# Attention's output matmuls in alternation with the piece next to them on TensorE

## The chip, the cores and the metric

The kernel runs on one core of a Trainium2 chip. The metric is the device time of one execution in microseconds (us); lower is better. Shorter times are in nanoseconds (ns).

## What is computed

Grouped-query attention followed by a feed-forward layer with a squared ReLU. There are 8 batches of 384 positions, 16 query heads on 4 key and value heads, and a head dimension of 64:

```
scores = q @ k.T / sqrt(64)                 # per batch and head, 384 x 384
attn   = exp(scores - max) / (sum(exp(scores - max)) + 1e-9)
x      = attn @ v                            # heads side by side: 3072 x 1024
h      = maximum(x @ w_in, 0)                # 1024 -> 2048
out    = (h * h) @ w_out                     # 2048 -> 1024
```

Inputs and output are float32; the kernel multiplies in 16-bit types.

## The kernel before

**Engines and recorder.** All work goes through `R.add(engine, fn, reads, writes, ...)` of the class `Recorder` (lines 22 to 170). It finds what an operation depends on and keeps it in one list; `emit` (L124) then writes each engine's operations in the order of their recording, a wait on semaphores before an operation and one increment at its last instruction. Loops that plan ahead (from about line 1640 on) choose what TensorE gets next, from modelled times at which operands and PSUM banks come free. So the order on TensorE (PE) is fixed when the kernel is built.

**Batches.** While the feed-forward layer of batch b runs on PE, attention of batch b + 1 runs between its pieces. Three kinds of piece matter:

- *score*, in `burst_small` (matmuls at L471): q times k for one or two key tiles, 512 or 256 columns, into two PSUM banks; ScalarE (ACT) takes the exponential from there (L481).
- *up* and *down*, built by `zipped` (matmuls at L926 for the first matrix, at L968 for the second; an older form of them, for batch 0, is at L634 and L1302). Both use a scheme of seven products for a 2 x 2 split. A piece has mostly eight matmuls, of 192 columns (up) or 512 (down).
- *attention's output*, in `av_halves` (matmuls at L538), for batches 1 to 6. For one pair of heads' results there are 36 matmuls, in two operations of 18, the halves: `mm(pe, 0)` and `mm(pe, 1)`. One matmul takes 65 columns: 64 of v, and a column of ones that gives the sum for the softmax. After the second half DVE takes the reciprocal (L551) and multiplies (L553), and the result goes by a transposing DMA (L558) to the next layer.

**Row halves.** Nearly all of these matmuls use 64 of the 128 rows of PE's array: half 0 or half 1, by the partitions that the operands are on. In the instruction order they alternate between the halves, so that two run side by side. A sum over 128 rows is made in two passes into the same PSUM bank: what half 0 has begun in a bank, half 1 continues later, and the other way round. The second waits by semaphore until the first has landed (`after=(lead,)` in `av_halves`, `lead` in `zipped`), so PE has waits on itself.

The two halves of an attention output, in the kernel before, order their matmuls by bank:

```
for x in range(2):
    f, h = 6 * s2 + NJ * x + n, (x + y) % 2
```

The first operation (y = 0) is 0, 1, 0, 1 in row halves, the second (y = 1) is 1, 0, 1, 0.

Of the kernel before, what the change touches and what calls it, by code (L numbers as in the profile page):

```python
# [8 lines left out]
class Tally:  # L9
# [5 lines left out]
    def __getattr__(self, name):  # L15
        def count(*args, **kwargs):
            self.n += 1
            return self
        return count


class Recorder:
# [37 lines left out]
            t = max(t, o["end"])  # L60
        return t

    def add(self, eng, fn, reads=(), writes=(), dma=None, cost=0.1, issue=0.1, shared=(), after=(), port=False):
        i = len(self.ops)
        deps = self.deps_of(reads, writes)
        raw = {self.writer[r] for r in reads if r in self.writer}
        for r in reads:
            self.readers.setdefault(r, []).append(i)
        for w in writes:
            self.writer[w] = i  # L70
            self.readers[w] = []
        need = set(after)
        for d in deps:
            o = self.ops[d]
            if o["dma"] is None and o["eng"] == eng and dma is None:
                if eng in self.IN_ORDER or d not in raw:
                    continue
            need.add(d)
        if dma is not None:
            if dma in self.dma_last:  # L80
                need.add(self.dma_last[dma])
            self.dma_last[dma] = i
        start = max([self.clock[eng]] + [self.ops[d]["end"] for d in need])
        if dma is not None:
            self.clock[eng] = start + issue
            if eng == "gpsimd":
                self.pool.append((start, start + 0.3 * issue))
            q = eng
            begin = max(self.ring.get(q, 0.0), start + issue + 0.8)
            if shared and begin > start + issue + 0.8:  # L90
                shared = (3.0, shared[1])
            if shared and self.ring.get("gpsimd", 0.0) > begin:
                self.ring["gpsimd"] += shared[1]
                for o in self.ops:
                    if o["eng"] == "gpsimd" and o["dma"] is not None and o["end"] > begin:
                        o["end"] += max(0.0, min(shared[1], o["end"] - 1.2 - begin))
                cost = shared[0]
            self.ring[q] = begin + cost
            kind = dma.rstrip("0123456789z_")
            lag, work = self.WIRE.get(kind, (2.2, 1.25))  # L100
            self.wire = max(self.wire, start + lag) + work
            end = begin + cost + (1.5 if begin > 30 else 1.2 if eng == "gpsimd" else 0.7)
        else:
            if eng == "gpsimd":
                self.pool.append((start, start + cost))
            elif port:
                cost += max([0.0] + [z - start for a, z in self.pool[-6:] if a <= start < z])
            self.clock[eng] = start + cost
            if eng == "tensor":
                fn(self.tally)  # L110
                self.marks.append((start + cost, self.tally.n))
            end = start + cost + (0.2 if eng == "tensor" else 0.07)
        self.ops.append(dict(eng=eng, fn=fn, dma=dma, need=need, signal=False, start=start, end=end))
        return i

    def emit(self):
        nc, ops = self.nc, self.ops
        for o in ops:
            for d in o["need"]:
                ops[d]["signal"] = True  # L120
        sems = {e: nc.alloc_semaphore(f"done_{e}") for e in self.ENGINES}
        count = {}
        for o in ops:
            if o["dma"] is not None:  # L124
                s = self.dma_sems.get(o["dma"])
                if s is None:
                    s = self.dma_sems[o["dma"]] = nc.alloc_semaphore(f"dma_{o['dma']}")
                key, step = ("dma", o["dma"]), 16
            elif o["signal"]:
                s, key, step = sems[o["eng"]], o["eng"], 1  # L130
            else:
                o["at"] = None
                continue
            count[key] = count.get(key, 0) + step
            o["at"] = (key, count[key])
            o["sem"] = s
        known = {e: {} for e in self.ENGINES}
        for o in ops:
            k = known[o["eng"]]
            waits = {}  # L140
            for d in sorted(o["need"], reverse=True):
                key, v = ops[d]["at"]
                if k.get(key, 0) >= v:
                    continue
                waits[key] = (ops[d]["sem"], v)
                for kk, vv in ops[d]["know"].items():
                    if k.get(kk, 0) < vv:
                        k[kk] = vv
                if k.get(key, 0) < v:
                    k[key] = v  # L150
            o["waits"] = [w for w in waits.values()]
            o["know"] = dict(k)
            if o["at"] is not None:
                o["know"][o["at"][0]] = max(o["know"].get(o["at"][0], 0), o["at"][1])
        with nc.Block() as block:
            for e in self.ENGINES:
                mine = [o for o in ops if o["eng"] == e]

                def body(eng, mine=mine):
                    for o in mine:  # L160
                        for s, v in o["waits"]:
                            eng.wait_ge(s, v)  # L162
                        last = o["fn"](eng)
                        if o["at"] is not None:
                            last.then_inc(o["sem"], 16 if o["dma"] is not None else 1)

                getattr(block, e)(body)

# [3 lines left out]
def bass_gqa_attention__then__ffn_squared_relu_kernel(  # L172
# [14 lines left out]
    NJ = S // 128  # L187
# [17 lines left out]
    R = Recorder(nc)  # L205
# [258 lines left out]
    def burst_small(b, pieces, base):  # L464

        n, c0, wide = slot(b, pieces[0][0]), pieces[0][1], pieces[0][2]

        def sc(pe):
            for m, (u, _, _) in enumerate(pieces):
                for x in range(2):  # L470
                    mm = pe.matmul(ps[:, base + x, m * wide:(m + 1) * wide],  # L471
                                   kT[at(b)][64 * x:64 * x + 64, u, :], q_cols(b, u // NJ, x, c0, c0 + wide))
            return mm

        total = wide * len(pieces)
        keys = [("bank", base), ("bank", base + 1)]
        R.add("tensor", sc, reads=[r for p in pieces for r in score_reads(b, *p)], writes=keys,
              cost=total / 2400 + (0.004 if b else 0.2))
        src = ps[:, base:base + 2, 0:total].rearrange("p x (k c) -> p x k c", k=len(pieces))
        dst = expT[n // 6][:, n % 6:n % 6 + len(pieces), :, c0:c0 + wide].rearrange("p k x c -> p x k c")  # L480
        R.add("scalar", lambda e: e.activation(dst, src, AF.Exp, scale=0.125), reads=keys,  # L481
              writes=[("expT", slot(b, u), t) for u, _, _ in pieces
                      for t in range(c0 // 128, (c0 + wide) // 128)], cost=(0.2 if b else 0.07) + total / 600)
# [41 lines left out]
    def av_halves(b, c, pairs):  # L525

        g, s2 = c // 2, c % 2
# [3 lines left out]
        def mm(pe, y):  # L531
            for n in range(NJ):
                for j in range(NJ):
                    for x in range(2):
                        f, h = 6 * s2 + NJ * x + n, (x + y) % 2
                        r = slice(64 * h, 64 * h + 64)
                        w = unit_of(b, g * NJ + j)[r, f % 2, (f // 2) * 128:(f // 2) * 128 + 128]
                        m = pe.matmul(ps[:, p[x], n * DP:n * DP + D + 1], w, v_aug[b % 2][r, g * NJ + j, 0:D + 1],  # L538
                                      start=(n + j + y == 0), stop=(n + j + y == 2 * NJ - 1))
            return m  # L540

        keys = [("bank", i) for i in p]
        lead = R.add("tensor", lambda pe: mm(pe, 0), reads=av_reads(b, c), writes=keys, cost=0.275)
        yield lead
        held.difference_update(p)
        R.add("tensor", lambda pe: mm(pe, 1), reads=av_reads(b, c), writes=keys, cost=0.275, after=(lead,))
        r = (b * 8 + c) % 2
        o = o_slot(b, g)
        po = ps[:, p[0]:p[0] + 2, 0:NJ * DP].rearrange("p s (i e) -> p s i e", i=NJ)
# [285 lines left out]
    def zipped(ups, lows):  # L835
# [15 lines left out]
        def piece():  # L851
            def mm(pe):
                for _, _, m in todo:
# [2 lines left out]

            held.update(first)
            i = R.add("tensor", mm, reads=need, writes=[("bank", x) for x in sorted({h.bank for h in halves})], cost=cost,
                      after=tuple(e[0] for h in halves for e in h.lead))
            for h in halves:  # L860
                if h.done:
                    h.done(i)
# [1166 lines left out]
```

## Time and profile before

| | |
|---|---|
| median of 3 runs | 395.71 us (394.32 to 395.84) |
| the profiled execution | 395.19 us, its span 393.4 us |
| PE matmuls | 387.3 us busy, 98% of the span, 7019 instructions |
| PE weight loads | 302.6 us, 77% |
| VectorE (DVE) | 308.3 us, 78% |
| ScalarE (ACT) | 272.2 us, 69% |
| GpSimd (POOL) | 144.6 us, 37% |
| granted TensorE clock | 0.999 |

A line of a group reads: source line, engine, operation, what is written and read, partitions x elements and type, the count; then the busy time in us, the mean of one in ns, and the idle time ahead of it with what ended it. `64*128 64x65` is a matmul over 64 rows and 128 columns of the array with 65 columns streamed through. PEld stands for the weight loads, which run beside the matmuls. Matmuls overlap: 190 ns is the time of one from start to end, not the distance between two. In a timeline the columns are start (us from the span's start), duration (us), engine, line, operation and operands; rows that follow each other closely are merged with a count.

### The profile page before, as it was taken

The numbers are of one execution on the slowest core, as the hardware profiler recorded it, in microseconds if no ns is written. First come the engines' busy times: TensorE is split into PE (matmuls) and PEld (weight loads), VectorE is DVE, ScalarE is ACT, GpSimd is POOL, SyncE is SP. The second block draws the span as 40 slices with busy tenths as digits, with TensorE's granted clock in tenths as the row PEclk, the third lists the DMA queues.
The fourth block names the chain that finished last, engine by engine and source line by source line (L and its number), as shares of the span: only waits on it lengthen the run. The fifth ranks groups of instructions, "written<-read, shape, count | busy, mean of one in ns | idle before, by whom it ended". The sixth has DMA issues, their size and how long they took to land. (4 is left out here: it accounts for less than half of the span.)

```text
span 393.4 us, 15642 instructions
## 1 busy us (share of the span) xinstructions
PE 387.3 (98%) x7019; PEld 302.6 (77%) x7022; DVE 308.3 (78%) x646; ACT 272.2 (69%) x397; POOL 144.6 (37%) x168
## 2 busy tenths in 40 slices
PE   8999999999999999999999999999999999999996
PEld 6565674455555899799977999899987899799653
DVE  3689788889989988888886688898885688856642
ACT  5948999689845897778882587978782297436511
POOL 7756420044002563466422243525301144126111
PEclk9999999999999999999999999999999999999999
DMA  9999999995329975884788318976712223120023
GB/s 168 182 197 188 207 200 181 147 258 82 42 77 125 188 103 79 126 158 77 107 125 186 105 25 73 139 145 83 83 49 102 86 45 25 48 82 4 28 82 107
DMA packets 95635, 44.40 MB, mean 113 GB/s; under 512 B 75984, under 2 KB 89552, under 8 KB 95568
## 3 DMA queue, kind: packets, MB, share of 16 engines
q0 software_dynamic: 36672, 17.44, 35.3%
q1 hardware_dynamic: 58080, 25.40, 32.4%
q8 instruction: 55, 0.90, 1.0%
q10 hardware_dynamic: 816, 0.56, 0.5%
q14 instruction: 12, 0.10, 0.1%
HBM read 35.65 MB, written 12.58 MB: 123 GB/s over the span
## 5 line engine op out<-in xcount | busy, mean ns | idle before, releaser
L481 ACT ACTIVATE expT<-ps 128x1024 bf16<-128x1024 f32 (+1 forms) x124 | 121.0, 1015 | 25.4 <-PE ps L471 25.1
L968 PE MATMUL ps<-w_out_sb,h2T 64*128 64x512 f16 x528 | 98.0, 376 | 0.0
L926 PE MATMUL ps<-xT,w_in_sb 64*128 64x192 f16 x1152 | 84.4, 243 | 0.3 <-DVE y_sb L1126 0.2
L926 PEld LDWEIGHTS ps<-xT,w_in_sb 64*128 64x128 f16 x1152 | 70.7, 94 | 3.0 <-PE ps L926 0.7
L823 POOL TENSOR_TENSOR h2T<-hr 128x384 f16<-128x384 f32 x55 | 44.8, 834 | 53.3 <-ACT hr L811 53.2
L968 PE MATMUL ps<-area,xT 64*128 64x512 f16 x288 | 55.7, 376 | 0.0
L926 PE MATMUL ps<-s_all,wx 64*128 64x192 f16 x768 | 52.0, 242 | 0.0
L471 PE MATMUL ps<-qT,kT 64*128 64x256 bf16 (+2 forms) x336 | 51.1, 326 | 0.5 <-ACT expT L481 0.4
L968 PEld LDWEIGHTS ps<-w_out_sb,h2T 64*128 64x128 f16 (+1 forms) x528 | 38.9, 94 | 16.1 <-ACT h2T L819 0.3
L811 ACT ACTIVATE hr<-hr,bits 128x384 f32<-128x384 f32 x72 | 42.6, 608 | 11.1 <-DVE hr L910 10.7
L1126 DVE SCALAR_TENSOR_TENSOR y_sb<-ps,bits,y_sb 128x512 f32<-128x512 f32 (+2 forms) x38 | 27.1, 725 | 24.1 <-PE ps L968 14.1
L910 DVE TENSOR_TENSOR hr<-ps,hr 128x384 f32<-128x384 f32 x72 | 39.3, 555 | 8.4 <-PE ps L926 5.1
L926 PEld LDWEIGHTS ps<-s_all,wx 64*128 64x128 f16 x768 | 44.0, 94 | 1.2
L538 PE MATMUL ps<-v_aug,expT 64*128 64x65 bf16 x1680 | 42.5, 190 | 0.1
L634 PE MATMUL ps<-xT,w_in_sb 64*128 64x384 bf16 x448 | 41.6, 323 | 0.6 <-DMA w_in_sb<-in_moe_w_in_dram 0.4
L1119 ACT ACTIVATE y_sb<-ps,bits 128x512 f32<-128x512 f32 x23 | 15.6, 687 | 36.9 <-PE ps L968 36.7
L538 PEld LDWEIGHTS ps<-v_aug,expT 64*128 64x128 bf16 x1680 | 39.0, 94 | 2.0 <-DVE o_sb L553 0.3
L1158 POOL TENSOR_TENSOR y_sb<-y_sb 128x512 f32<-128x512 f32 x9 | 11.6, 1290 | 65.7 <-DVE y_sb L1126 65.7
L968 PE MATMUL ps<-area,h2T 64*128 64x512 f16 x144 | 35.6, 376 | 0.0
L634 PEld LDWEIGHTS ps<-xT,w_in_sb 64*128 64x128 bf16 x448 | 22.1, 94 | 15.2 <-issue 1.5
L926 PE MATMUL ps<-xT,wx 64*128 64x192 f16 x384 | 32.5, 242 | 0.0
L926 PE MATMUL ps<-s_all,w_in_sb 64*128 64x192 f16 x384 | 32.4, 242 | 0.0
(146 smaller groups left out, 743.8 us busy)
## 6 DMA issues: line engine op xcount, KB each, us to landing
out_dram<-y_sb SPq DMA_DIRECT2D x45, 256.0 KB, 2.5
w_in_sb<-in_moe_w_in_dram POOLq DMA_DIRECT2D x8, 512.0 KB, 15.0
w_out_sb<-in_moe_w_out_dram POOLq DMA_DIRECT2D x4, 1024.0 KB, 29.0
q_st<-in_q_dram POOLq DMA_DIRECT2D x19, 192.0 KB, 5.1
q_st<-in_q_dram POOLq DMA_DIRECT2D x4, 384.0 KB, 23.7
k_st<-in_k_dram POOLq DMA_DIRECT2D x6, 192.0 KB, 4.3
k_st<-in_v_dram POOLq DMA_DIRECT2D x5, 192.0 KB, 4.8
wx<-in_q_dram POOLq DMA_DIRECT2D x2, 384.0 KB, 8.7
```

The costliest lines, as they stand in the source:

```text
L471: mm = pe.matmul(ps[:, base + x, m * wide:(m + 1) * wide], kT[at(b)][64 * x:64 * x + 64, u, :], q_cols(b, u // NJ, x, c0, c0 + wide))
L481: R.add("scalar", lambda e: e.activation(dst, src, AF.Exp, scale=0.125), reads=keys, writes=[("expT", slot(b, u), t) for u, _, _ in pieces ...
L538: m = pe.matmul(ps[:, p[x], n * DP:n * DP + D + 1], w, v_aug[b % 2][r, g * NJ + j, 0:D + 1], start=(n + j + y == 0), stop=(n + j + y == 2 ...
L634: m = pe.matmul(bank(4 + xs[x])[:, 0:S], w_in_sb[r, kc, c * 128:(c + 1) * 128], xT[b % NXT][r, kc, :], start=(phase < 2 and kc == 0), stop ...
L811: R.add("scalar", lambda e, val=val, to=to: e.activation(val, val, AF.Relu, scale=to), reads=[("hr", r)] + by, writes=[("hr", r)], cost=0. ...
L823: n = R.add(eng, lambda e, dst=dst, two=two: e.tensor_tensor(dst, two, two, ALU.mult), reads=[("hr", r)], writes=keys, cost=0.77 if other ...
L910: R.add("vector", lambda e: e.tensor_tensor(hr[r][:, :], src, hr[r][:, :], ALU.add), reads=[("bank", at), ("hr", r)], writes=[("hr", r)], ...
L926: return lambda pe: pe.matmul(bank(at)[:, f * h:f * h + h], w[r, kc, c:c + 128], m[r, kc, :], start=(prod in (1, 5, 2) and y + f + kc == 0 ...
L968: return lambda pe: pe.matmul(bank(p.at)[:, 0:512], p.a(k, r), p.w(k, r), start=start, stop=stop, skip_group_check=True)
L1119: R.add(eng, lambda e: e.activation(y_sb[y], bank(at), AF.Copy, scale=gs[g]) if eng == "scalar" else e.tensor_scalar(y_sb[y], bank(at), gs ...
L1126: R.add("vector", lambda e: e.scalar_tensor_tensor(y_sb[z][:, c0:c1], bank(at)[:, c0:c1], gs[g], y_sb[y][:, c0:c1], ALU.mult, ALU.add), re ...
L1158: R.add("gpsimd", lambda e: e.tensor_tensor(y_sb[z], y_sb[z], y_sb[y], ALU.add), reads=[("y", y), ("y", z)], writes=[("y", z)], cost=1.28)
```

## The change

The recorder's operations get a mark, `mix`: "a" on both halves of an attention output, "p" on score pieces from batch 2 on and on every piece of `zipped`. When the instructions of PE are written out, an "a" and a "p" that stand next to each other become one group and their matmuls are given in turn, two matmuls of the one, two of the other, spread over the length of both. The operation that is recorded first comes first; its waits stand ahead of the group, the other's waits ahead of its own first matmul, and each signals after its own last matmul. An "a" joins the "p" behind it if there is one, otherwise the "p" ahead of it if that is not yet in a group. Two operations stay apart where the second needs the first. In the second half of an attention output the order becomes 0, 1, 0, 1 in row halves as well.

```diff
+class Tape:
+    def __init__(self):
+        self.calls = []
+    def __getattr__(self, name):
+        def call(*args, **kwargs):
+            self.calls.append((name, args, kwargs))
+            return self
+        return call
...
+                def woven(eng, a, p):
+                    ta, tp = Tape(), Tape()
+                    a["fn"](ta)
+                    p["fn"](tp)
+                    ca, cp = [[t.calls[i:i + 2] for i in range(0, len(t.calls), 2)] for t in (ta, tp)]
+                    turns = sorted([(n / len(ca), 0, x) for n, x in enumerate(ca)] + [((n + 1.0) / len(cp), 1, x) for n, x in enumerate(cp)],
+                                   key=lambda x: x[:2])
+                    left, begun = [len(ca), len(cp)], False
+                    waits(eng, a)
+                    for _, side, x in turns:
+                        if side and not begun:
+                            waits(eng, p)
+                            begun = True
+                        last = play(eng, x)
+                        left[side] -= 1
+                        if not left[side]:
+                            signal((a, p)[side], last)
+
+                def apart(a, p):
+                    return a["at"] is not None and any(ops[d] is a or ops[d]["know"].get(a["at"][0], 0) >= a["at"][1] for d in p["need"])
+
                 def body(eng, mine=mine):
-                    for o in mine:
-                        for s, v in o["waits"]:
-                            eng.wait_ge(s, v)
-                        last = o["fn"](eng)
-                        if o["at"] is not None:
-                            last.then_inc(o["sem"], 16 if o["dma"] is not None else 1)
+                    groups, i = [], 0
+                    while i < len(mine):
+                        a, p = mine[i], (mine + [None])[i + 1]
+                        if a["mix"] == "a" and p and p["mix"] == "p" and not apart(a, p):
+                            groups.append((a, p))
+                            i += 1
+                        elif a["mix"] == "a" and groups and len(groups[-1]) == 1 and groups[-1][0]["mix"] == "p" and not apart(groups[-1][0], a):
+                            groups[-1] += (a,)
+                        else:
+                            groups.append((a,))
+                        i += 1
+                    for g in groups:
+                        if len(g) == 2:
+                            woven(eng, *g)
+                            continue
+                        waits(eng, g[0])
+                        signal(g[0], g[0]["fn"](eng))
...
-        R.add("tensor", sc, reads=[r for p in pieces for r in score_reads(b, *p)], writes=keys,
+        R.add("tensor", sc, mix="p" if b > 1 else None, reads=[r for p in pieces for r in score_reads(b, *p)], writes=keys,
...
-                    for x in range(2):
-                        f, h = 6 * s2 + NJ * x + n, (x + y) % 2
+                    for h in range(2):
+                        x = (h + y) % 2
+                        f = 6 * s2 + NJ * x + n
...
-        lead = R.add("tensor", lambda pe: mm(pe, 0), reads=av_reads(b, c), writes=keys, cost=0.275)
+        lead = R.add("tensor", lambda pe: mm(pe, 0), reads=av_reads(b, c), writes=keys, cost=0.275, mix="a")
...
-        R.add("tensor", lambda pe: mm(pe, 1), reads=av_reads(b, c), writes=keys, cost=0.275, after=(lead,))
+        R.add("tensor", lambda pe: mm(pe, 1), reads=av_reads(b, c), writes=keys, cost=0.275, after=(lead,), mix="a")
...
-                      after=tuple(e[0] for h in halves for e in h.lead))
+                      after=tuple(e[0] for h in halves for e in h.lead), mix="p")
```

With nine pairs of a half and four of a piece the turns are: half first, `a a a p a a p a a p a a p`; piece first, `p a a p a a p a a p a a a`. With a piece of one pair, half first, the order is as it was.

More of the change, by code (lines that the diff above doesn't have):

```diff
@@ L61, in when, with add @@
         return t
-    def add(self, eng, fn, reads=(), writes=(), dma=None, cost=0.1, issue=0.1, shared=(), after=(), port=False):
+    def add(self, eng, fn, reads=(), writes=(), dma=None, cost=0.1, issue=0.1, shared=(), after=(), port=False, mix=None):
         i = len(self.ops)
@@ L112, in add @@
             end = start + cost + (0.2 if eng == "tensor" else 0.07)
-        self.ops.append(dict(eng=eng, fn=fn, dma=dma, need=need, signal=False, start=start, end=end))
+        self.ops.append(dict(eng=eng, fn=fn, dma=dma, need=need, signal=False, start=start, end=end, mix=mix))
         return i
@@ L157, in emit, with waits @@
                 mine = [o for o in ops if o["eng"] == e]
-                def body(eng, mine=mine):
-                    for o in mine:
-                        for s, v in o["waits"]:
-                            eng.wait_ge(s, v)
-                        last = o["fn"](eng)
-                        if o["at"] is not None:
-                            last.then_inc(o["sem"], 16 if o["dma"] is not None else 1)
+                def waits(eng, o):
+                    for s, v in o["waits"]:
+                        eng.wait_ge(s, v)
@@ new lines, in signal, with play @@
+                def signal(o, last):
+                    if o["at"] is not None:
+                        last.then_inc(o["sem"], 16 if o["dma"] is not None else 1)
+                def play(eng, calls):
+                    for name, args, kwargs in calls:
+                        last = getattr(eng, name)(*args, **kwargs)
+                    return last
+                def woven(eng, a, p):
[15 more added lines that the diff above has]
+                            signal((a, p)[side], last)
```

## The prediction

> **What bounds the kernel now.** I read the page first: its span line, then the engines' busy times, then the group that the change moves.
>
> ```profile
> span 393.4 us, 15642 instructions
> PE 387.3 (98%) x7019; PEld 302.6 (77%) x7022; DVE 308.3 (78%) x646; ACT 272.2 (69%) x397; POOL 144.6 (37%) x168
> L538 PE MATMUL ps<-v_aug,expT 64*128 64x65 bf16 x1680 | 42.5, 190 | 0.1
> ```
>
> PE is busy in 98% of the span and every other engine in less than 80%, so a microsecond that PE loses or wins anywhere before the tail arrives at the end. The attention outputs are L538: 1728 matmuls with the 48 that read another tile, in 96 halves of 18. Each counts 190 ns, but they overlap, so their price has to come from starts. Next I asked for PE's waits between 99 and 335 us, the stretch in which all halves lie; they show in the weight loads:
>
> ```profile
> PEld ps L926 <- PE ps L926: 0.4, 1, 0.4
> PEld ps L926 <- DVE y_sb L1327: 0.4, 1, 0.4
> PEld ps L538 <- DVE o_sb L553: 0.3, 1, 0.3
> PEld ps L471 <- ACT expT L481: 0.3, 1, 0.3
> PEld ps L538 <- PE ps L538: 0.2, 1, 0.2
> ```
>
> Some 1.6 us of waits in 236 us: there is little idle time to win back, only the step between matmuls. Two kinds of release matter: other engines, and PE itself (a second half of a sum waits until its first half has landed). Third, PE's timeline, for the steps:
>
> ```profile
> 150.66 0.24 PE L926 MATMUL ps<-s_all,w_in_sb 64*128 64x192 f16 x1
> ...
> 151.32 0.45 PE L538 MATMUL ps<-v_aug,expT 64*128 64x65 bf16 x18
> 151.60 0.24 PE L926 MATMUL ps<-s_all,w_in_sb 64*128 64x192 f16 x1
> ...
> 153.46 0.37 PE L968 MATMUL ps<-w_out_sb,h2T 64*128 64x512 f16 x1
> ...
> 154.32 0.45 PE L538 MATMUL ps<-v_aug,expT 64*128 64x65 bf16 x16
> ```
>
> From 150.66 to 151.32 lie eight pairs of 192 columns: 82.5 ns a pair. From 153.46 to 154.32 lie four of 512: 215 ns. The half at 151.32 ends after 0.28 us: nine pairs at 31 ns. Entering and leaving it costs nothing that the starts show.
>
> **What moves.** The order in which the programs' instructions stand is the same on DVE, ACT, POOL and SP; only PE's differs. Of the 96 halves 11 stay alone and 18 meet a score piece of one pair, which the rule puts behind all nine: no new order. The other 67 are interleaved, nearly all half first: three narrow pairs, one wide, then two and one in turn, the last wide pair last. Three groups stand piece first. Nothing is added or dropped; planner, buffers and queues are as they were.
>
> **Term 1, the step.** Between 192 and 512 columns the price is (215 - 82.5) / 320 = 0.414 ns a column, so 65 columns would take 82.5 - 127 x 0.414 = 29.9 ns if only streaming counted. A half has 31.1 at the mean of its rows, so something (weight loads, I take it) costs 1.2 ns, and a wide neighbour could hide at most that: 67 x 9 x 1.2 = 0.7 us gain. A change of width could as well cost up to 1 ns, some 0.5 us. I take -0.3: each weight load starts only when the matmul ahead of it in its row half starts (the half at 151.32 loads first at 151.24, with the last wide pair), so a narrow pair still has to cover one load, whatever follows.
>
> **Term 2, PE's waits on itself.** The price of such a wait is seen at 134.37: 18 pairs run to 135.16 where 18 x 31 = 0.56, so 0.23 is idle at the change of halves: from the last narrow start to the first that needs it 0.26 us pass, 0.19 of them the matmul, 0.07 the signal. For a 192-column matmul that makes 0.24 + 0.07 = 0.31. Now a batch's first up piece:
>
> ```profile
> 309.69 0.32 PE L926 MATMUL ps<-xT,w_in_sb 64*128 64x192 f16 x2
> 309.83 0.47 PE L538 MATMUL ps<-v_aug,expT 64*128 64x65 bf16 x18
> 310.12 0.51 PE L926 MATMUL ps<-xT,w_in_sb 64*128 64x192 f16 x8
> 310.45 0.47 PE L538 MATMUL ps<-v_aug,expT 64*128 64x65 bf16 x19
> ```
>
> The piece at 310.12 accumulates on what the matmuls at 309.69 began. The second of these starts at 309.77, so it may start from 309.77 + 0.31 = 310.08. The half between them covers this to 0.04 us. Interleaved, the piece is due after three pairs, at 309.83 + 0.09 = 309.92, and PE stands 0.16 us, with the remaining six narrow pairs queued behind the wait. This occurs at five batch starts (near 128, 168, 219, 259 and 310 us): 0.8. The second half at 310.45 waits for the last pair of the first, which now stands one wide pair before it: due 0.031 + 0.083 = 0.11 after it, ready after 0.26, so 0.15. The same happens near 219.9 and 259.3, where it stays alone: 0.45. Near 192.7 and 155.0 a second half follows its group directly: 0.2 and 0.1. Together 1.55 us. The idle 0.23 at 134.37 stays, since its first half is placed last in its group. Elsewhere a whole piece (0.33) or a score lies between, which covers 0.31.
>
> **Term 3, waits on other engines.** A half that used to end before its piece now ends beside it. Near 104 us:
>
> ```profile
> 103.69 0.44 PE L538 MATMUL ps<-v_aug,expT 64*128 64x65 bf16 x18
> 104.40 0.56 DVE L553 TENSOR_TENSOR o_sb<-ps,bits 128x384 f16<-128x384 f32 x1
> 105.26 0.38 PE L471 MATMUL ps<-qT,kT 64*128 64x512 bf16 x2
> ```
>
> The half's last pair gets three 512-wide pairs ahead of it, 0.65 us. DVE's reciprocal and the product at 104.40 go later by as much and end at 105.61; the score at 105.26 waits for the bank that they free: with the signal 105.68, a stall of 0.4. Near 116 us the half comes second: it waits for the exponential that ACT ends at 115.81, and now is due after one 512-wide pair of its piece and not after four, 0.65 earlier. It had 0.2 to spare (it started at 116.09), so up to 0.45 with the rest of the piece behind it; I take 0.4. Slack of other such waits is mostly over 0.2 us against 0.19 by which pieces come forward, and evictions of a piece end no later than before, since its last pair stays last; I put 0.2 on the few with less (near 140 and 151.6). Term 3: 1.0 us; bounds 0.3 (scores and exponentials shift with PE and take half of it back) and 2.0.
>
> **The sum.** -0.3 + 1.55 + 1.0 = +2.25 us. The profiled execution took 395.19, 1.8 outside the span, which nothing here touches: 397.4. It lies 0.5 below the median of the three runs, 395.71; what I forecast is a median, so 397.9, which is 0.57% over it. Half a per cent, 2 us, is about what a measurement of this kernel can tell from no change.
>
> **Rivals.** *The planner's slack takes the waits* (not slower). PE's 1.6 us of waits speak for margins; each stall moves PE back, and the next release is then early. If term 2 falls to 0.6 (only what has 0.04 of cover) and term 3 to 0.3 while the whole 0.7 is hidden, the sum is +0.2: 395.9. It decides if a released piece is mostly ready by the third narrow pair, 0.09 us in. Against it: the cover of 0.04 at 310.08, the same at five places. Chance 0.25.
>
> *The two row halves keep strict order.* In four pieces near 192, 243, 283 and 334 one half streams 512 columns and the other 192. If no matmul may start ahead of an earlier one of the other half, each of three entries of narrow pairs makes one half wait 0.215 - 0.083 = 0.13: 4 x 3 x 0.13 = 1.6 more, 399.5. Against it, two rows of the timeline:
>
> ```profile
> 176.47 0.24 PE L926 MATMUL ps<-xT,w_in_sb 64*128 64x192 f16 x1
> 176.48 0.19 PE L538 MATMUL ps<-v_aug,expT 64*128 64x65 bf16 x1
> ```
>
> The wide matmul stands behind all 18 in the program and starts before the last. That shows a lead of one place, not of several. Chance 0.12. The Trainium skill, "TensorE: Matmul & The Clock Gate", section "Part 3: Packing small matmuls — row/col tiling", says that matmuls start and end in program order without reordering. By that rule the time would be this rival's; the trace differs by these 10 ns.
>
> *Narrow pairs vanish beside wide ones* (faster). 67 x 0.28 = 18.8 us stand in the halves; over 2 us net would need a third of the step to be hidden. The step is already within 1.2 ns of streaming. Chance 0.05, some 393.
>
> **How the numbers follow.** The waits as priced, 0.58: 396.9 to 399, three quarters of it over 397.7. So slower 0.44 + 0.12 = 0.56, same 0.14 + 0.25 = 0.39, faster 0.05. Range: from the first rival's low side (395.3) to the second's with terms 1 and 3 at their bad ends (400.7).
>
> **What would show it.** Right: PE waits on itself at the five batch starts, 0.15 to 0.2 each, on weight loads of the interleaving line, and a score near 105 that waits for DVE; half groups of four 192-wide pairs that take 0.33 + 0.28 us where nothing waits. Wrong: groups much shorter than 0.61 (term 1), no self waits (term 2), or a PE that idles in new places by over 3 us.

## The result and the profile after

The changed kernel takes 396.9 us (median of 11 runs, 396.22 to 397.7) against 395.27 us (11 runs, 394.18 to 395.89) of the kernel before: a ratio of 1.0048, 95% interval 1.0034 to 1.0063. It is slower by half a per cent, 1.9 us by the ratio and 1.6 between the medians. Run again later (e7 below) it gave 1.0072, 1.0058 to 1.0086. The two intervals meet near 1.006, 2.4 us.

The page of the changed kernel, the lines that answer to the three shown of before (L538 is now L182 where an operation is alternated and L597 where it stands alone; L182 also holds the up, down and score matmuls of the groups; L471 became L529, L481 L539, L551 L610, L553 L612, L926 L985, L968 L1027; in e1 to e4 all of these but L182 stand 8 lines further down):

```profile
span 394.8 us, 15642 instructions
PE 388.4 (98%) x7019; PEld 291.6 (74%) x7022; DVE 309.0 (78%) x646; ACT 272.2 (69%) x397; POOL 145.2 (37%) x168
L182 PE MATMUL ps<-v_aug,expT 64*128 64x65 bf16 x1506 | 57.3, 190 | 0.4 <-ACT expT L539 0.3
```

The engines' counts and the mean of 190 ns are those of before (57.3 us for L538's 42.5, because the same matmuls now lie between others). A busy share of 98% in both cannot show where 2 us went, so the reading rests on two other views.

The first is the distance on PE's timeline between two rows that the change does not touch: the first attention output after 98 us, ahead of the first group, and the last group of 384-column matmuls. The counts and durations of the first row are cut where the stretch asked for, 97 to 99.6 us, ends; its start is what is read. Before, then after:

```profile
99.14 0.63 PE L538 MATMUL ps<-v_aug,expT 64*128 64x65 bf16 x30
388.16 1.92 PE L1023 MATMUL ps<-w_out_sb,xT 128*128 128x384 f16 x16
```

```profile
98.13 1.00 PE L597 MATMUL ps<-v_aug,expT 64*128 64x65 bf16 x54
389.58 1.92 PE L1082 MATMUL ps<-w_out_sb,xT 128*128 128x384 f16 x16
```

289.02 us before, 291.45 after: the stretch with the groups is **2.43 us longer**. The part ahead of it was 1.01 us shorter in this execution, although no instruction there is moved; 2.43 - 1.01 = 1.42 is the difference of the two spans (394.8 and 393.4). For every kernel below, span and distance fit together in this way, so the distance is the cleaner measure, nearly free of what the opening does from one execution to the next (e1 has an exception).

The second view is PE's waits between 99 and 337 us, by its weight loads:

```profile
PEld ps L529 <- DVE o_sb L612: 1.2, 3, 0.7
PEld ps L182 <- ACT expT L539: 1.0, 2, 0.7
PEld ps L597 <- PE ps L182: 0.5, 3, 0.2
```

The first two kinds are new against before's list, and the third stood there once, with 0.2 (L538 on itself). They count idle time of the load engine, which stops ahead of the matmuls, so they overstate a stall: the 0.7 of a score on DVE and the 0.7 of a half on ACT cost PE 0.41 and 0.42 us, as the starts below show. And they miss stalls at which the next loads had already been made: those at the batch starts do not stand here at all. So I compared the start of each unmoved PE instruction in both traces. Counted from 95 us, the delay grows in steps: 0.50 us by 106, 0.91 by 119, 1.22 by 157, 1.39 by 170, 1.88 by 222, 2.20 by 262, 2.45 by 313 (times of before's trace), and 2.43 at the end. Between the steps it is flat to some hundredths. Nothing that is lost is made good later.

The batch start near 311 us on PE's timeline, to set beside the rows at 309.69 to 310.45 of before:

```profile
310.83 0.33 PE L985 MATMUL ps<-xT,w_in_sb 64*128 64x192 f16 x2
310.99 0.26 PE L182 MATMUL ps<-v_aug,expT 64*128 64x65 bf16 x6
311.23 0.26 PE L182 MATMUL ps<-xT,w_in_sb 64*128 64x192 f16 x2
...
311.67 0.24 PE L182 MATMUL ps<-xT,w_in_sb 64*128 64x192 f16 x2
311.89 0.46 PE L597 MATMUL ps<-v_aug,expT 64*128 64x65 bf16 x18
```

Three narrow pairs from 310.99 are done by 310.99 + 0.09 = 311.08; the up piece starts at 311.23. **PE stands 0.15 us** for the matmuls of 310.83, and the other six narrow pairs stand behind that wait. Then the next half, L597, is due one wide pair after 311.67, at 311.75, and starts at 311.89: **0.14 us**, for the last narrow pair of the group.

Near 104 us a score waits for the bank that DVE frees, with DVE late because its half was alternated with a down piece:

```profile
103.89 0.61 PE L1027 MATMUL ps<-w_out_sb,h2T 64*128 64x512 f16 x4
104.12 0.56 DVE L612 TENSOR_TENSOR o_sb<-ps,bits 128x384 f16<-128x384 f32 x1
104.73 0.60 PE L529 MATMUL ps<-qT,kT 64*128 64x512 bf16 x4 [0.24 <-DVE o_sb L612]
```

DVE ends at 104.68, the score starts 0.05 later. It was due two wide pairs after 103.89, 104.32: a stall of 0.41. Near 115 us a half comes second in its group and waits for an exponential, and the piece that it is alternated with stands too:

```profile
114.27 1.02 ACT L539 ACTIVATE expT<-ps 128x1024 bf16<-128x1024 f32 x1 [0.44 <-PE ps L529]
114.71 0.38 PE L182 MATMUL ps<-w_out_sb,h2T 64*128 64x512 f16 x2
115.35 0.24 PE L182 MATMUL ps<-v_aug,expT 64*128 64x65 bf16 x4 [0.26 <-ACT expT L539]
```

ACT ends at 115.29. The half was due one wide pair after 114.71, at 114.93, and starts at 115.35: 0.42.

### The profile page after: what moved, and what is told of

Its sections match the earlier page's. It is cut to its first block, busy times and chain, and to the rows that moved or that the text cites. A ratio compares the mean times of both kernels' runs of the same rounds, so it can differ in the third digit from the quotient of the medians.

```text
span 394.8 us, 15642 instructions
## 1 busy us (share of the span) xinstructions
PE 388.4 (98%) x7019; PEld 291.6 (74%) x7022; DVE 309.0 (78%) x646; ACT 272.2 (69%) x397; POOL 145.2 (37%) x168
## 5 line engine op out<-in xcount | busy, mean ns | idle before, releaser
L539 ACT ACTIVATE expT<-ps 128x1024 bf16<-128x1024 f32 (+1 forms) x124 | 121.0, 1017 | 25.3 <-PE ps L529 18.2
L1027 PE MATMUL ps<-w_out_sb,h2T 64*128 64x512 f16 x453 | 86.8, 376 | 0.0
L985 PE MATMUL ps<-xT,w_in_sb 64*128 64x192 f16 x960 | 71.2, 243 | 0.3 <-DVE y_sb L1185 0.2
L985 PEld LDWEIGHTS ps<-xT,w_in_sb 64*128 64x128 f16 x960 | 60.6, 94 | 2.6 <-PE ps L985 0.7
L182 PE MATMUL ps<-v_aug,expT 64*128 64x65 bf16 x1506 | 57.3, 190 | 0.4 <-ACT expT L539 0.3
L1027 PE MATMUL ps<-area,xT 64*128 64x512 f16 x288 | 55.5, 376 | 0.0
L182 PEld LDWEIGHTS ps<-v_aug,expT 64*128 64x128 bf16 x1506 | 50.6, 94 | 4.5 <-ACT expT L539 1.0
L1027 PEld LDWEIGHTS ps<-w_out_sb,h2T 64*128 64x128 f16 (+1 forms) x453 | 34.6, 94 | 15.8 <-ACT h2T L878 0.3
L985 PE MATMUL ps<-s_all,wx 64*128 64x192 f16 x660 | 44.2, 243 | 0.0
L529 PE MATMUL ps<-qT,kT 64*128 64x256 bf16 (+2 forms) x284 | 40.9, 320 | 0.8 <-ACT expT L539 0.4
L985 PEld LDWEIGHTS ps<-s_all,wx 64*128 64x128 f16 x660 | 37.8, 94 | 1.9
L1027 PE MATMUL ps<-area,h2T 64*128 64x512 f16 x138 | 34.0, 376 | 0.0
L961 ACT COPY hr<-ps 128x384 f32<-128x384 f32 x33 | 15.5, 481 | 24.2 <-PE ps L182 13.9
L1027 PE MATMUL ps<-w_out_sb,xT 64*128 64x512 f16 x128 | 31.5, 376 | 0.0
```

The lines of the kernel that those rows point to most:

```text
L182: last = getattr(eng, name)(*args, **kwargs)
L529: mm = pe.matmul(ps[:, base + x, m * wide:(m + 1) * wide], kT[at(b)][64 * x:64 * x + 64, u, :], q_cols(b, u // NJ, x, c0, c0 + wide))
L961: R.add("scalar", lambda e: e.copy(hr[r][:, :], src), reads=[("bank", at)], writes=[("hr", r)], cost=0.45, after=hr_read.pop(r, ()))
L985: return lambda pe: pe.matmul(bank(at)[:, f * h:f * h + h], w[r, kc, c:c + 128], m[r, kc, :], start=(prod in (1, 5, 2) and y + f + kc == 0 ...
L1027: return lambda pe: pe.matmul(bank(p.at)[:, 0:512], p.a(k, r), p.w(k, r), start=start, stop=stop, skip_group_check=True)
```

## The experiments

All seven start from the changed kernel. e1 to e4 alternate a chosen part of the groups. For that an operation knows its number (`i`), and `mix` tells an up piece ("pu") from one with 512-column matmuls ("pd") and from a score ("ps"); `q` is the operation ahead of the pair on PE, `z` the one behind it. The rule that forms a group then reads:

```diff
-                        if a["mix"] == "a" and p and p["mix"] == "p" and not apart(a, p):
-                            groups.append((a, p))
-                            i += 1
+                        q, z = mine[i - 1] if i else None, mine[i + 2] if i + 2 < len(mine) else None
+                        if a["mix"] == "a" and p and is_p(p) and not apart(a, p):
+                            lead = q is not None and q["i"] in p["need"]
+                            follow = z is not None and a["i"] in z["need"]
+                            if CHOOSE:
+                                groups.append((a, p))
+                                i += 1
+                            else:
+                                groups.append((a,))
```

`lead` is true where the piece continues sums of the operation just ahead, `follow` where the operation behind the pair continues those of the half: the two forms of term 2. An "a" that joins the piece ahead of it does so in e4 alone, and there only with a "pd". The measurements together, e1 to e4 on one chip (before there: 394.70 us, 34 runs), e5 to e7 on another (394.72 us, 11 runs):

| kernel | groups | median us | ratio to before, 95% interval | opening against before | distance against before |
|---|---|---|---|---|---|
| changed kernel, first profile | 66 | 396.90 | 1.0048 (1.0034 to 1.0063) | -1.01 | +2.43 |
| e1_halves | 0 | 394.49 | 1.0003 (0.9990 to 1.0016) | -0.45 | +0.24 |
| e2_covered | 27 | 394.59 | 1.0002 (0.9989 to 1.0014) | -0.92 | -0.14 |
| e3_own_waits | 9 | 396.18 | 1.0039 (1.0028 to 1.0050) | -1.28 | +1.61 |
| e4_down | 11 | 395.53 | 1.0013 (1.0001 to 1.0025) | -0.79 | +0.81 |
| e5_late | 66 | 395.91 | 1.0031 (1.0019 to 1.0043) | -0.65 | +1.36 |
| e6_early | 66 | 397.59 | 1.0071 (1.0057 to 1.0084) | -0.18 | +2.97 |
| e7_again | 66 | 397.67 | 1.0072 (1.0058 to 1.0086) | +0.34 | +2.43 |

Opening is the start of the first row (99.14 before), distance that from it to the last row (289.02 before), each from one profile, in us. In every row the interval of the time holds the distance; the profile tells the places.

**e1_halves: only the order of the row halves.** `CHOOSE` is `False`: no group, but the second half of each attention output has the changed kernel's order 0, 1, 0, 1.

> No alternation at all: every operation stands whole, as before. Only the second half of each attention output has its row halves in the order 0, 1 instead of 1, 0. Theory W (the change costs its new waits, 1.55 us on PE itself and some 0.9 us on DVE and ACT, and its step gains 0.1): no difference, within 0.2 us of before. Rival O (the order of the row halves is what costs): +1 to +2 us. Rival S (alternation itself makes the steps longer): no difference here.

The time is that of before. The distance is 0.24 us longer, and 0.30 of that arise at one wait that exists before as well, near 129 us, for DVE's y_sb: in the list of load waits it is 0.7 here and 0.4 before. DVE starts on y_sb at 128.19 here and at 128.33 before, which is 0.30 later counted from PE's first row. Why is not shown. The new order of the halves is not the reason, since e2, e3 and e4 have it too and list 0.3, 0.2 and 0.4 for this wait. Apart from it the distance is before's to 0.06. The reordered halves are free, so the loss belongs to the alternation.

**e2_covered: only groups that get no new wait.** Up pieces that wait for nothing but PE, are not started by the operation just ahead, and whose half is not needed by the one just behind:

```diff
-                            if CHOOSE:
+                            if p["mix"] == "pu" and own(p) and not lead and not follow:
```

> Alternation in 27 groups only, with up pieces of 192 columns whose waits are on PE alone and lie further back than the operation ahead, and where the next operation does not need the half: nothing new to wait for. Theory W: 27 x -2.3 ns = -0.06 us, the same time as before within 0.3 us, and in the trace no PE wait that before does not have. Rival S: 27 of 66 groups, so 27/66 of what the change costs, +0.7 us or more, spread evenly over the groups.

27 groups, and the time of before:

```profile
98.22 1.28 PE L605 MATMUL ps<-v_aug,expT 64*128 64x65 bf16 x72
387.10 1.92 PE L1090 MATMUL ps<-w_out_sb,xT 128*128 128x384 f16 x16
```

288.88 against 289.02 us: a gain of 5 ns a group at most, and 0.06 us of it is what e1 has without any group. Alternating with up pieces neither costs nor gains anything that the time shows. The slow part is not the step between matmuls.

**e3_own_waits: only groups of term 2.** The groups at which PE must wait for itself, the first up pieces of five batches and four groups that are followed at once by the second half of the same output. Two of these four, near 100 and 102 us, are not in the prediction's list:

```diff
-                            if CHOOSE:
+                            if p["mix"] == "pu" and lead or follow:
```

> Alternation in 9 groups only: the first up piece of five batches (it continues a sum that the operation just ahead began), and groups that are followed at once by the second half of the same output. Theory W: five stalls of 0.16, three of 0.15 at second halves that directly follow, 0.2 and 0.1 near 192.7 and 155: +1.5 us (1.2 to 1.8), nearly two thirds of the change from a seventh of its groups, seen as PE waiting for PE. Rival S: 9/66, +0.2 us.

Nine of 66 groups bring 1.61 us of the 2.43, and 1.0039 in time. The steps of the delay against before lie near 102 us (0.06), 130 (0.13), 155 (0.09), 168 (0.16), 193 (0.19), 220 (0.35), 260 (0.33) and 311 (0.31), and in the waits a half that stands alone (L605) waits for a group (L182):

```profile
PEld ps L605 <- PE ps L182: 0.9, 6, 0.2
```

This is what the rival in which the planner's slack takes the waits denies. It falls: 0.2 was asked by it for the whole change.

**e4_down: only the pieces with 512-column matmuls.** Here lie the two stalls on DVE and ACT, and three of the four groups in which one row half streams 512 columns and the other 192 (near 243, 283 and 334 us):

```diff
-                            if CHOOSE:
+                            if p["mix"] == "pd" and not follow:
```

> Alternation in 11 groups only, those with pieces that hold 512-column matmuls, without the ones of the run on own waits. Theory W: a score near 105 us waits for DVE by 0.4 us more, a half near 116 us waits for the exponential by 0.4, the mixed pieces near 243, 283 and 334 cost nothing: +0.8 us (0.6 to 1.0), all of it before 118 us. Rival S: 11/66, +0.3 us, spread to 334 us. Rival of strict order between row halves: +0.4 at each of the three mixed pieces.

The distance is 0.81 us longer; the time 0.5 (interval 0.04 to 1.0). Both stalls are there (0.41 and 0.42) and make the 0.81; the other nine groups change the delay by 0.04 at most, so the alternation itself is free with 512 columns too. There is no step near 243, 283 or 334. From the first 512-column matmul of the down piece near 283 to the first of the next one:

```profile
282.40 0.38 PE L1035 MATMUL ps<-w_out_sb,h2T 64*128 64x512 f16 x1
...
282.61 0.22 PE L182 MATMUL ps<-v_aug,expT 64*128 64x65 bf16 x2
282.65 0.24 PE L993 MATMUL ps<-xT,wx 64*128 64x192 f16 x1
282.68 0.37 PE L182 MATMUL ps<-w_out_sb,h2T 64*128 64x512 f16 x1
282.74 0.22 PE L182 MATMUL ps<-v_aug,expT 64*128 64x65 bf16 x2
...
283.75 0.38 PE L1035 MATMUL ps<-w_out_sb,h2T 64*128 64x512 f16 x1
```

1.35 us here; in before's trace the same two start at 282.35 and 283.76, 1.41. By the prediction's price, strict order would have added 0.13 at each of three entries. The starts show directly that the order is not kept between the row halves. The 192-column matmul at 282.65 (L993) is the last of the operation ahead of the group, and two narrow ones behind it start 0.04 us earlier. The 512-column one at 282.68 stands behind the two narrow ones of 282.74 and starts 0.06 earlier. So that rival falls: mixed widths on the two row halves do not hold each other up. Before's trace had this too: two narrow matmuls at 282.57, and behind them in time, at 282.61, a 192-column one that stands ahead of them; the rival needed no run. The Trainium skill, "TensorE: Matmul & The Clock Gate", section "Part 3: Packing small matmuls — row/col tiling", says that matmuls start and end in program order. At the rival's price that would have made this run 1.2 us slower at these three groups; the run shows none of it, and the starts above are out of that order.

**e5_late: the second operation in the latter half of the first.** If the stalls are due times that come too early, giving the second operation's matmuls later must shrink them with nothing else changed:

```diff
-                    turns = sorted([(n / len(ca), 0, x) for n, x in enumerate(ca)] + [((n + 1.0) / len(cp), 1, x) for n, x in enumerate(cp)],
+                    turns = sorted([(n / len(ca), 0, x) for n, x in enumerate(ca)] + [(0.5 + 0.5 * (n + 1.0) / len(cp), 1, x) for n, x in enumerate(cp)],
```

> The same 66 groups alternate, but the second operation's pairs are spread over the latter half of the turns (a a a a a a p a p a p a p): its first pair is due after six narrow pairs, not three. Theory W: the due time decides. The five stalls at the batches' first up pieces shrink by 3 x 0.031 = 0.09 us each, from 0.17 to 0.08; the half near 116 us, that stands second in its group, is due two 512-wide pairs later (0.43), and its stall of 0.42 vanishes; the score near 105 (0.4) and the second halves (0.15 each) stay. In the trace from 95 us to the end +1.5 us against before, where the change has 2.4; as a time 0.7 to 1.0 less than the change. Rival S (every alternation costs): as many changes of width as in the change, so the same time as the change.

With all 66 groups in place the loss falls from 2.43 to 1.36 us. At the last batch start:

```profile
310.21 0.32 PE L985 MATMUL ps<-xT,w_in_sb 64*128 64x192 f16 x2
310.37 0.36 PE L182 MATMUL ps<-v_aug,expT 64*128 64x65 bf16 x12
310.60 0.26 PE L182 MATMUL ps<-xT,w_in_sb 64*128 64x192 f16 x2
...
310.95 0.25 PE L182 MATMUL ps<-xT,w_in_sb 64*128 64x192 f16 x2
311.18 0.30 PE L597 MATMUL ps<-v_aug,expT 64*128 64x65 bf16 x8
```

The piece now comes after six narrow pairs, 310.37 + 0.19 = 310.56, and starts at 310.60: 0.04 where the changed kernel stands 0.15. The half at 311.18 still waits 0.15 (due at 310.95 + 0.08 = 311.03), since the group's end is as it was. The stall near 115 us is gone from the delay, the one near 104 us stays. In time e5 is 1.8 us below e7 on the same chip, where 0.7 to 1.0 was expected: 1.07 is in the distance, and the opening of e7's profile is 0.99 later than e5's.

**e6_early: the second operation's first pair right behind the first narrow pair.** The opposite dose:

```diff
-                    turns = sorted([(n / len(ca), 0, x) for n, x in enumerate(ca)] + [((n + 1.0) / len(cp), 1, x) for n, x in enumerate(cp)],
+                    turns = sorted([(n / len(ca), 0, x) for n, x in enumerate(ca)] + [((n + 1.0) / len(cp) if n or len(cp) < 2 else 0.05, 1, x) for n, x in enumerate(cp)],
```

> The same 66 groups, but the second operation's first pair is given after one narrow pair, not three; the rest of the turns as in the change. Theory W: the five stalls at the batches' first up pieces grow by 2 x 0.031 = 0.06 us, from 0.17 to 0.23, so +0.3 us against the change, and perhaps 0.1 more at pieces that wait for DVE near 130 and 151.6. In the trace +2.7 to 2.9 from 95 us to the end. Rival S: the same time as the change.

The distance grows to +2.97 (2.7 to 2.9 expected), 0.54 over the changed kernel. The stall at each of the five batch starts is 0.06 us longer, as expected. The five batch starts, hidden in the changed kernel's list, now stand in the waits, each for the matmuls (L985) just ahead:

```profile
PEld ps L182 <- PE ps L985: 1.0, 5, 0.2
```

In time, 397.59 against e7's 397.67 us, the 0.54 us does not show; the openings of the two profiled executions differ by as much (0.52). This step rests on the traces alone.

**e7_again: the changed kernel, unaltered.** Another profile and other runs of the same program.

> The changed kernel once more, unaltered, beside the two others on the same chip: +1.6 us against before, by the runs so far (1.3 to 2.5), and in its trace +2.4 from 95 us to the end if the waits are the cause; a different stretch before 95 us, where nothing is moved, would show how much of a single execution's time is drift of the opening.

The distance is 2.43 us longer once more, with the same steps. But the opening is 0.34 us later than before's where the first profile's was 1.01 earlier, and so one span is 396.2 and the other 394.8 us. The time, 2.8 us over before by the ratio, lies above the 1.3 to 2.5 expected. The difference between the two profiled executions lies in the stretch that the change does not touch; whether that between 1.0048 and 1.0072 does too is not shown. Why that stretch differs between executions was not studied.

## Why the prediction was right, point by point

- **Direction and size.** +2.25 us was forecast. The trace shows +2.43 twice, the two measurements, by their ratios, +1.9 (1.3 to 2.5) and +2.8 (2.3 to 3.4). The three terms err by 0.16, 0.06 and -0.04 against the trace, so the sum is not right by luck.
- **Count of groups.** 66 are alternated, not 67. It changes nothing.
- **Term 1, the step: too large.** It took a gain of 0.3 us. Over 39 groups of up pieces that wait for nothing, the time from the half's first start to the first start behind the group is 609.5 ns before and 607.5 after: 2 ns a group, 0.14 us over 66. The rows are those predicted:

```profile
149.53 0.26 PE L182 MATMUL ps<-v_aug,expT 64*128 64x65 bf16 x6
...
150.14 0.25 PE L985 MATMUL ps<-s_all,w_in_sb 64*128 64x192 f16 x2
```

  149.53 to 150.14 is 0.61, the forecast 0.33 + 0.28. Two narrow pairs between wide ones take 62 to 65 ns, 31 each: a wide neighbour hides next to nothing of the 1.2 ns that the estimate gave to weight loads. The reason given, that a narrow pair still covers one load, fits this but was not tested by itself.
- **Term 2, PE's waits on itself: right.** 1.55 forecast, 1.61 in e3, of which 0.06 are the two groups that its list lacks. At the five batch starts PE stands 0.12 to 0.15 us in the changed kernel (0.16 forecast), at the second halves near 220, 260 and 311 us 0.14 (0.15). Near 193 and 155 us the steps in e3 are 0.19 and 0.09 (0.2 and 0.1). The price behind it, from the start of the last matmul that is needed to the first that needs it, is 0.30 to 0.33 us for 192 columns (0.31 forecast) and 0.25 to 0.26 for 65 (0.26) at these places: 310.92 + 0.31 = 311.23 above.
- **Term 3, other engines: right.** 1.0 forecast. What is left of 2.43 without terms 1 and 2 is 2.43 + 0.14 - 1.61 = 0.96: 0.41 near 104 us and 0.42 near 115 us (0.4 each forecast, e4 shows the two alone), and 0.13 near 151.6, where a piece waits for DVE (0.2 forecast for the smaller ones).
- **What would show it.** "PE waits on itself at the five batch starts, ... on weight loads of the interleaving line" was right in the matmuls' starts, and wrong as a view: the list of load waits does not show them in the changed kernel, as the loads of the next matmuls were already made.
- **Rivals.** The planner's slack took none of it (e3: 1.61 us where 0.6 was asked of term 2). Strict order of the row halves is not kept (e4); the prediction saw a lead of one place in before's trace and took the rival to be open. Narrow pairs did not vanish beside wide ones (e2: time of before).
- **Reference time.** The prediction stood on the median of three runs, 395.71; with the 395.27 of the later runs the same sum gives 397.5. The choice cost 0.4 us, more than the sum's own error against the trace, 0.18. The median forecast, 397.9, is 1.0 above the 396.9 measured: 0.4 is this choice, and 0.6 is +2.25 against the +1.63 between the medians, less than the openings of two executions differ by.

## What to carry to other kernels

Alternating two operations does not only mix their instructions: it brings every wait of the second forward and every completion of the first back, by up to the length of the other, and a wait then holds both. Before interleaving, list for each pair who produced what the second needs and who consumes the first's result, with the cover in nanoseconds that the present order gives. Here 11 of 66 groups (nine of e3, two of e4) carried nearly all of the loss, and 27 of the others, run by themselves, neither lost nor won, since the step between matmuls stayed within 2 ns a group of what it was.

## What the runs showed of the hardware that was not expected

- The stretch ahead of about 98 us, with the same PE instructions in all kernels, started the first row of the table between 1.28 us earlier and 0.34 us later than before's profile, and twice differently for one and the same kernel (e7 and the first profile, 1.35 us apart). Behind it the same program repeated its delay to 0.01 us. A difference of two profiled spans is thus good to about a microsecond here, one between two inner rows to hundredths in this pair; in e1 a single wait for DVE moved it by 0.30.
- 192-column and 512-column matmuls on the two row halves, with 65-column pairs between them, ran without a loss that the trace shows (1.35 against 1.41 us), and one half's matmuls started up to 0.06 us ahead of matmuls of the other half that stand before them in the program (282.68 against 282.74).
